# Transposing v as 32-bit words of two channels in a cross-covariance attention and highway kernel

## The chip, the cores and the metric

The kernel runs on one core of a Trainium2 chip. A core has TensorE (PE), which multiplies matrices and can transpose, and whose loads of the stationary operand are recorded apart (PEld); VectorE (DVE); ScalarE (ACT); GpSimd (POOL); SyncE (SP), which here only starts transfers; and 16 DMA engines. Each engine works through its own queue in order. The metric is the device time of one execution in microseconds (us), and smaller is better.

## The reference

Four batches, 6336 positions (N), 256 channels (C), everything f32 in memory. Attention is between channels, so its map is only 256 x 256 for each batch, and a highway layer follows.

```python
qn = q / (norm(q, axis=1) + 1e-06)          # norm of each channel over N
kn = k / (norm(k, axis=1) + 1e-06)
a  = softmax(kn.transpose(0, 2, 1) @ qn / tau)   # (B, 256, 256)
x  = (v @ a).reshape(B * N, 256)
H  = maximum(x @ w_h, 0)
T  = sigmoid(x @ w_t + b_t)
out = T * H + (1 - T) * x                   # (25344, 256)
```

## The kernel before

**Tiles.** A batch is 49 tiles of 128 positions and a rest of 64. q, k and v are loaded by POOL-issued transfers that cast f32 to f16, in groups of 2 to 13 tiles (QG, VG), into rings of 4 buffers for q and k each and 3 for v.

**Scores.** For each tile, `emit_score` multiplies k's two halves of channels (stationary, 128 weights each) with all 256 channels of q into a sum S (line 230). The norms are the diagonals of Gram matrices G: k's halves with themselves (line 234) and q's halves with themselves (line 239), two matmuls of 128 columns for each. For some runs of four tiles, listed in RUNS, the sum of squares is made without PE instead (`make_run`): ACT squares (line 448), POOL adds halves (454), DVE reduces (461), and `pe_sums` (511) adds the result to G by an f32 matmul with ones at the end of the batch.

**Chain.** When a batch's scores are complete, `make_chain` goes through norms (502), logits (557), exponentials (574), softmax (588), a transpose of the map, a product with w_h and w_t (618), and copies (629) into `mr`, an f16 tile of 768 columns: for each row, which is a channel of k, the map and its products with w_h and w_t. So x, H's argument and T's argument are all v times a part of `mr`.

**Slots.** An output slot is a pair of position tiles; a batch has 25, the last one with the rest of 64. For each slot PE transposes v, four times 128 x 128 in f16 (line 293, `emit_transpose`), into one PSUM bank (tag vT, a single buffer), DVE or ACT copies it to the SBUF tile `vts` (line 307, or 305 for the slot with the rest; ACT_COPY lists the slots that ACT copies), and `mains` multiplies three times four: `vts` as stationary, 256 columns of `mr` moving (line 317), for the sigmoid's argument (zbank, seeded with the bias by an ACT copy, 361), for H and for x. ACT makes the sigmoid (358), DVE two products (366, 376), POOL most of the final subtractions (399), and stores go out from SP (415) in groups of four slots.

**Order.** A planner in the same file writes the order of every queue: tasks with lengths and dependencies are put on the engines step by step, and the program is emitted in that order. On PE the chain goes first, then scores that are due (S_END, SAHEAD), then transposes up to LOOKS slots ahead, then mains. TAIL says for how many last tiles of a batch Gram products go ahead of scores; QOFF and VOFF how early loads are put in POOL's order; OUTST how many loads may be under way; HOLD how many full output buffers are held back before stores go out; NEAR when DVE prefers a copy; LASTS_AT where the last batch's slot with the rest stands. The lengths that the planner uses for a task (TR, copies) only shape the order.

Of the kernel before, what the change touches and what calls it, by code (L numbers as in the profile page):

```python
# [11 lines left out]
f32 = mybir.dt.float32  # L12
f16 = mybir.dt.float16
u16 = mybir.dt.uint16

P = 128
# [44 lines left out]
def kernel(  # L61
# [11 lines left out]
    nc = tc.nc  # L73

    B, N, C = q.shape
# [11 lines left out]
    def spans(*sizes):  # L87
# [10 lines left out]
    GT = {"q": 12, "k": 12, "v": 13}  # L98
    CH = 4
    SQR = {"q": 4, "k": 2}  # L100
    RUNS = {1: {'q': [4, 8, 20, 32, 36, 44], 'k': [0, 8, 24, 28, 32, 40]}, 2: {'q': [0, 8, 12, 16, 20, 24, 28, 36, 40], 'k': [0, 12, 16, 32, 40]}, 3: {'q': [8, 12, 20, 28, 32, 40, 44], 'k': [0, 8, 16, 28, 32, 36]}}
    TAIL = [6, 12, 10, 7]
    SPARE = 0
    QOFF, VOFF = [1.5, 3.0, 4.0, 0.5], [7.5, 3.5, 0.5, 9.5]
    SAHEAD = [0, 0.5, 10.0, 10.5]
    LOOKS = [3, 3, 2, 2]
    HOLD = [2, 1, 1, 5]
    DVE_SUBS = 2
    SINGLES = 8
    ACT_COPY = {3, 14, 21, 22, 26, 34, 36, 39, 40, 44, 45, 51, 53, 54, 58, 61, 63, 64, 72, 77, 81, 83, 84, 88, 91, 96, 98, 99}  # L110
    NEAR = 2
    OUTST = 7
    QRING, VRING, ORING = 4, 3, 7
    TTR, UXR, VTR = 4, 3, 5
    OG = 4
    LASTS_AT = 18
    LASTS = list(range(LASTS_AT)) + [NPAIR - 1] + list(range(LASTS_AT, NPAIR - 1))
    PAIRS = [list(range(NPAIR))] * (B - 1) + [LASTS]
    S_END = [21.5, 42.5, 65.0]

    ctx.enter_context(tc.manual_schedule())
    const_pool = ctx.enter_context(tc.tile_pool(name="consts", bufs=1))
# [1 line left out]
    work_pool = ctx.enter_context(tc.tile_pool(name="work", bufs=2))  # L124
    psum_pool = ctx.enter_context(
        tc.tile_pool(name="psum", bufs=1, space=bass.MemoryType.PSUM)
    )
# [9 lines left out]
    for t in range(NSLOT):  # L137
        b, i = pair_of(t)
# [13 lines left out]


    MM = lambda n: n / 2376.0 + 0.0025
    EXP_LAG = 0.6
    PE_LAG, LAG, TO_PE = 0.20, 0.08, 0.10
    TILE = 0.309
    STEP, LAND = 0.01, 0.9
# [60 lines left out]
    def emit_score(b, j, parts, first, last):  # L219
        if first:  # L220
            tags = ("S", "G") if b == 0 else ("hx1", "hx2")
            S_t[b] = psum_pool.tile([P, 2, C], f32, tag=tags[0], name=f"S{b}")
            G_t[b] = psum_pool.tile([P, 4, P], f32, tag=tags[1], name=f"G{b}")
        nr = REM if j == NS else P
        kk, qq = tile_of("k", b, j), tile_of("q", b, j)
        S, G = S_t[b], G_t[b]
        for c in range(2):
            kc = kk[0:nr, bass.ts(c, P)]
            if "s" in parts:
                nc.tensor.matmul(  # L230
                    S[:, c, :], kc, qq[0:nr, :], start=first and c == 0, stop=last and c == 1
                )
            if "k" in parts:
                nc.tensor.matmul(  # L234
                    G[:, c, :], kc, kc, start=begins(b), stop=False, skip_group_check=True,
                )
        for c in range(2 if "q" in parts else 0):
            qc = qq[0:nr, bass.ts(c, P)]
            nc.tensor.matmul(  # L239
                G[:, 2 + c, :], qc, qc, start=begins(b), stop=False, skip_group_check=True  # L240
            )
# [42 lines left out]
    vT_ps, vT_t = {}, {}  # L284
    slot_of = {pair_of(t): t for t in range(NSLOT)}

    def emit_transpose(t):
        b, i = pair_of(t)
        ps = psum_pool.tile([P, 2, 2, P], f16, tag="vT", name=f"vtps{t}")
        for u, r in enumerate(nrows(i)):  # L290
            vt = tile_of("v", b, 2 * i + u)
            for c in range(2):
                nc.tensor.transpose(  # L293
                    ps[:, u, c, 0:r], vt[0:r, bass.ts(c, P)], ident[0:r, 0:r]
                )
        vT_ps[t] = ps

    def emit_copy(t, e):
        i = pair_of(t)[1]
        sb = work_pool.tile([P, 2, 2, P], f16, tag="vTs", bufs=VTR, name=f"vts{t}")  # L300
        cp = nc.vector.tensor_copy if e == "DVE" else nc.scalar.copy
        ps = vT_ps.pop(t)
        if i == NPAIR - 1:
            for u, r in enumerate(nrows(i)):
                cp(out=sb[:, u, :, 0:r], in_=ps[:, u, :, 0:r])
        else:
            cp(out=sb, in_=ps)  # L307
        vT_t[t] = sb

    mr_t = {}  # L310

    def mains(t, dst, off, seeded):
        b, i = pair_of(t)
        mr = mr_t[b]
        for u, r in enumerate(nrows(i)):
            for kt in range(2):
                nc.tensor.matmul(  # L317
                    dst[0:r, u, :], vT_t[t][:, u, kt, 0:r], mr[:, kt, off : off + C],
                    start=(not seeded and kt == 0 and (u == 0 or i == NPAIR - 1)),
                    stop=(kt == 1 and (u == 1 or i == NPAIR - 1)),  # L320
                    skip_group_check=seeded,
                )
# [169 lines left out]
    def make_chain(b):  # L492
        st = {}
        T = {}
        def norms(kind):
# [9 lines left out]
                    )  # L505
            return emit

        def pe_sums(e):
            for kind, o in (("q", 2), ("k", 0)):
                for c in range(2 if (kind, b) in sums_t else 0):  # L510
                    nc.tensor.matmul(
                        G_t[b][:, o + c, :],
                        areas[kind][sums_t[kind, b]][:, 0, bass.ts(c, P)], ones32,
                        start=False, stop=True, skip_group_check=True,
                    )

# [202 lines left out]
    for t in range(NSLOT):  # L719
        i = pair_of(t)[1]  # L720
        odd = i == NPAIR - 1
        Z[t] = Task(("Z", t), "PE", 4 * MM(C), lambda e, t=t: mains(t, zbank[t % 2], 2 * C, True))

        def emit_hx(e, t, which):
            task = (H if which == "h" else X)[t]
            hx[which, t] = bank_tile(task, f"{which}{t}")
            mains(t, hx[which, t], C if which == "h" else 0, False)

        H[t] = Task(("H", t), "PE", 4 * MM(C), lambda e, t=t: emit_hx(e, t, "h"))
        X[t] = Task(("X", t), "PE", 4 * MM(C), lambda e, t=t: emit_hx(e, t, "x"))  # L730
        H[t].wants_bank = X[t].wants_bank = True
        H[t].readers = lambda t=t: [TH[t]]
        X[t].readers = lambda t=t: [UX[t]]
        TR[t] = Task(("T", t), "PE", 4 * MM(P), lambda e, t=t: emit_transpose(t))
        CP[t] = Task(("C", t), "any", 0.0, lambda e, t=t: emit_copy(t, e))
        TT[t] = Task(("tt", t), "ACT", 0.61, lambda e, t=t: emit_tt(t))
        SEED[t] = Task(("seed", t), "ACT", 0.61, lambda e, t=t: emit_seed(t))
        TH[t] = Task(("th", t), "DVE", 0.75 if odd else 0.61, lambda e, t=t: emit_th(t))
        UX[t] = Task(("ux", t), "DVE", 0.75 if odd else 0.61, lambda e, t=t: emit_ux(t))
# [247 lines left out]
    def take(n, engine, now, length=None):  # L987
        task = head(n)
        if not can(task, now):
            return False  # L990
        if engine == "PE" and slot_now() == 0 and last_score[0].end is not None:
            if any(t.engine == "DMA" and t.end + LAND + 0.5 > now for t, _ in task.after):
                return False
        ptr[n] += 1
        run(task, engine, now, length)
        return True

    def soon(engine, now, length):
        task = head(engine + ".chain")
        if task is None or task.name[1] not in (0, B - 1):  # L1000
            return False
        if any(t.end is None for t, _ in task.after):
            return False
        return max(t.end + lag for t, lag in task.after) < now + length
# [31 lines left out]
    def step_act(now):  # L1036
        for n in ("ACT.chain", "ACT.tt", "ACT.seed"):
            if (n != "ACT.tt" or not exp_table()) and take(n, "ACT", now):
                return True
        wait = slot_now() == 0 and soon("ACT", now, 0.58)  # L1040
        if not wait and ptr["copy"] in ACT_COPY and take("copy", "ACT", now, 0.58):
            return True
        return slot_now() > 0 and not soon("ACT", now, 1.05) and take("ACT.sq", "ACT", now)

    def step_dve(now):
        if take("DVE.chain", "DVE", now):
            return True
        if slot_now() == 0 and soon("DVE", now, 0.42):
            return False
        mine = ptr["copy"] not in ACT_COPY  # L1050
        if mine and ptr["copy"] - slot_now() < NEAR and take("copy", "DVE", now, 0.42):
            return True
        if take("DVE.thux", "DVE", now) or take("DVE.sub", "DVE", now):
            return True
        if mine and take("copy", "DVE", now, 0.42):
            return True
        return slot_now() > 0 and not soon("DVE", now, 1.0) and take("DVE.red", "DVE", now)

# [122 lines left out]
```

## Time and profile before

| | |
|---|---|
| median of 3 runs | 270.83 us (270.56 to 274.89) |
| profiled execution | 270.55 us, span 268.8 us |
| PE, PEld busy | 246.3 us (92%), 213.7 us (79%) |
| DVE, ACT, POOL busy | 207.6, 192.9, 206.5 us |
| read from, written to memory | 78.4 MB, 26.0 MB |
| transposes of v (line 293) | 392 of 128x128 and 8 of 64 rows, f16 |
| mains (line 317) | 1200 |
| runs of squares (line 448) | 39, 1055 ns each on ACT |

PE is one of TensorE's rows, PEld the other; they overlap. A busy row says when an engine was at work, not that it was at its peak: matmuls are pipelined, and what one costs is the distance of its start from the next. A group's line ends in busy us, mean ns of one, and the idle time before it with what ended it. The DMA line gives the mean busy share of the 16 DMA engines in tenths.

### The profile page before, as it was taken

What the parts mean: (1) busy time and instruction counts of PE and PEld (TensorE: products, weight loads), DVE (VectorE), ACT (ScalarE), POOL (GpSimd) and SP (SyncE); (2) the same over time, 40 slices, a digit from 0 to 9 for tenths busy, and PEclk for the clock granted to TensorE, in tenths of its full rate; (3) what the DMA queues carried; (4) which work ended last, traced back from release to release, by engine and by line L of the source; (5) the groups of instructions that cost most, each with busy time, mean ns of one, the idle gap of its engine ahead of it and who ended that gap; (6) DMA issues with size and microseconds to landing.
All of it is one profiled execution on the core that took longest, in us unless ns stands there. A gap on an engine that the chain in (4) does not pass through costs nothing.

```text
span 268.8 us, 6452 instructions
## 1 busy us (share of the span) xinstructions
PE 246.3 (92%) x2564; PEld 213.7 (79%) x2564; DVE 207.6 (77%) x414; ACT 192.9 (72%) x320; POOL 206.5 (77%) x183
## 2 busy tenths in 40 slices
PE   0996886999999999989999999999999999999990
PEld 0696784798889997879989987898988687999780
DVE  2000035869999999889989899889998998999894
ACT  3310025969689978879996798898868987888780
POOL 6133455399989999898899998899966485977880
PEclk9999999999999999999999999999999999999998
DMA  7999999999999999999999999999999999698435
GB/s 215 213 214 212 205 186 212 214 209 220 213 210 213 235 266 220 209 274 213 288 290 307 278 213 226 214 297 302 272 291 356 266 408 399 142 235 355 200 129 215
DMA packets 16143, 66.08 MB, mean 246 GB/s; under 512 B 1777, under 2 KB 4338, under 8 KB 13170
## 3 DMA queue, kind: packets, MB, share of 16 engines
q0 software_dynamic: 11040, 38.67, 73.0%
q1 hardware_dynamic: 4786, 26.22, 24.3%
q10 hardware_dynamic: 288, 0.79, 0.8%
q8 instruction: 20, 0.33, 0.4%
q14 instruction: 9, 0.07, 0.1%
HBM read 78.38 MB, written 25.95 MB: 388 GB/s over the span
## 4 chain that ended last, share of the span: by engine, by line
PE 47%; DMA 29%; POOL 9%; DVE 7%; ACT 3%; issue 3%; DVEq 0%; POOLq 0%; ACTq 0%
DMA k<-in_k_dram 24%; PE x L317 10%; PE h L317 9%; PE zbank L317 9%; PE S L230 7%; PE vtps L293 5%; POOL o L399 4%; DMA out_dram<-o 3%; PE G L234 3%; PE G L239 3%; DVE o L366 2%; DMA qk<-in_k_dram 2%; DVE ux L376 2%; ACT tt L358 1%; POOL q L177 1%
## 5 line engine op out<-in xcount | busy, mean ns | idle before, releaser
L399 POOL TENSOR_TENSOR o<-o,ux 128x1024 f32<-128x1024 f32 (+2 forms) x50 | 111.5, 2233 | 23.4 <-DVE ux L376 20.3
L317 PEld LDWEIGHTS <-vts 128*128 128x128 f16 x1200 | 111.7, 98 | 16.2 <-issue 4.1
L230 PE MATMUL S<-q,k 128*128 128x256 f16 x392 | 73.5, 278 | 12.5 <-ACT k L834 6.3
L358 ACT ACTIVATE tt<-zbank 128x512 f32<-128x512 f32 x100 | 59.4, 596 | 22.0 <-PE zbank L317 15.7
L366 DVE SCALAR_TENSOR_TENSOR o<-h,tt 128x512 f32<-128x512 f32 x96 | 65.6, 684 | 6.0 <-ACT tt L358 3.3
L376 DVE SCALAR_TENSOR_TENSOR ux<-tt,x 128x512 f32<-128x512 f32 (+1 forms) x104 | 68.0, 657 | 2.1 <-PE x L317 2.0
L317 PE MATMUL x<-mr,vts 128*128 128x256 f16 (+1 forms) x400 | 60.5, 273 | 0.3 <-DVE o L366 0.3
L317 PE MATMUL zbank<-mr,vts 128*128 128x256 f16 (+1 forms) x400 | 60.6, 273 | 0.0
L317 PE MATMUL h<-mr,vts 128*128 128x256 f16 (+1 forms) x400 | 60.5, 273 | 0.0
L361 ACT COPY zbank<-btb 128x512 f32<-128x512 f32 x98 | 57.6, 591 | 2.7
L230 PEld LDWEIGHTS <-k 128*128 128x128 f16 x392 | 37.5, 100 | 18.9 <-DMA k<-in_k_dram 7.8
L234 PE MATMUL G<-k 128*128 128x128 f16 x256 | 44.0, 224 | 0.7 <-DVE junk L502 0.7
L293 PE MATMUL vtps<-ident,v 128*128 128x128 f16 x392 | 38.3, 219 | 1.5 <-DVE vts L307 0.7
L307 DVE COPY vts<-vtps 128x512 f16<-128x512 f16 x68 | 28.6, 420 | 7.2 <-PE vtps L293 6.7
L293 PEld LDWEIGHTS <-v 128*128 128x128 f16 x392 | 28.7, 98 | 4.9 <-issue 1.7
L177 POOL DMA_DIRECT2D q<-in_q_dram x25 | 14.2, 570 | 23.0 <-PE G L239 18.6
L502 DVE SCALAR_TENSOR_TENSOR junk<-G,ident 128x128 f32<-128x128 f32 x16 | 4.7, 291 | 31.1 <-PE G L234 30.4
L239 PE MATMUL G<-q 128*128 128x128 f16 x216 | 28.6, 224 | 0.0
L454 POOL TENSOR_TENSOR sqq<-sqq 128x512 f32<-128x512 f32 (+1 forms) x22 | 26.5, 1207 | 0.1
L234 PEld LDWEIGHTS <-k 128*128 128x128 f16 x256 | 24.0, 101 | 1.8 <-issue 1.1
L448 ACT ACTIVATE sqq<-q 128x1024 f32<-128x1024 f16 x22 | 23.0, 1055 | 0.1
L461 DVE TENSOR_REDUCE sqq<-sqq 128x256 f32<-128x768 f32 x22 | 22.6, 1026 | 0.0
(78 smaller groups left out, 214.3 us busy)
## 6 DMA issues: line engine op xcount, KB each, us to landing
out_dram<-o SPq DMA_DIRECT2D x23, 1024.0 KB, 9.8
v<-in_v_dram POOLq DMA_DIRECT2D x11, 768.0 KB, 17.2
q<-in_q_dram POOLq DMA_DIRECT2D x7, 768.0 KB, 15.2
k<-in_k_dram POOLq DMA_DIRECT2D x7, 768.0 KB, 19.3
q<-in_q_dram POOLq DMA_DIRECT2D x9, 512.0 KB, 13.4
k<-in_k_dram POOLq DMA_DIRECT2D x9, 512.0 KB, 15.4
v<-in_v_dram POOLq DMA_DIRECT2D x4, 832.0 KB, 19.1
q<-in_q_dram POOLq DMA_DIRECT2D x4, 256.0 KB, 13.2
```

The lines of the kernel that those rows point to most:

```text
L230: nc.tensor.matmul(S[:, c, :], kc, qq[0:nr, :], start=first and c == 0, stop=last and c == 1)
L234: nc.tensor.matmul(G[:, c, :], kc, kc, start=begins(b), stop=False, skip_group_check=True,)
L239: nc.tensor.matmul(G[:, 2 + c, :], qc, qc, start=begins(b), stop=False, skip_group_check=True)
L293: nc.tensor.transpose(ps[:, u, c, 0:r], vt[0:r, bass.ts(c, P)], ident[0:r, 0:r])
L307: cp(out=sb, in_=ps)
L317: nc.tensor.matmul(dst[0:r, u, :], vT_t[t][:, u, kt, 0:r], mr[:, kt, off : off + C], start=(not seeded and kt == 0 and (u == 0 or i == NPA ...
L358: nc.scalar.activation(out=tts[t], in_=zbank[t % 2], func=Act.Sigmoid)
L361: nc.scalar.copy(out=zbank[t % 2], in_=btb)
L366: nc.vector.scalar_tensor_tensor(out=ot[pr, o0 + us.start : o0 + us.stop, :], in0=hx["h", t][pr, us, :], scalar=0.0, in1=tts[t][pr, us, :] ...
L376: nc.vector.scalar_tensor_tensor(out=uxs[n][pr, 2 * half + us.start : 2 * half + us.stop, :], in0=tts[t][pr, us, :], scalar=1.0, in1=hx["x ...
L399: ins = sub.tensor_tensor(out=dst, in0=dst, in1=uxs[n][pr, us, :], op=AluOp.subtract)
L454: nc.gpsimd.tensor_tensor(out=sq[:, 1 : 1 + half, :], in0=sq[:, 1 : 1 + half, :], in1=sq[:, 1 + CH - half : 1 + CH, :], op=AluOp.add,)
```

## The change

v's f16 tile is read as 32-bit words, each of two neighbouring channels, and transposed by f32 transposes with the f32 identity `ident0`: one 128 x 128 transpose for each position tile instead of two. A row of the result then belongs to a channel pair, and a position's two channels lie side by side. The copy moves 256 f32 words instead of 512 f16 values, and its result is viewed as f16 again. The mains read their stationary operand with a step of two elements, and contract over even channels first, then odd ones. So that `mr` has its rows in that order, k's channels are taken with a step of two in the scores and Grams and in the sums of squares. RUNS lists 30 runs instead of 39 (by the change's own title 27). Planner constants are others: lengths of transposes and copies, and all that places work.

```diff
-    RUNS = {1: {'q': [4, 8, 20, 32, 36, 44], 'k': [0, 8, 24, 28, 32, 40]}, 2: {'q': [0, 8, 12, 16, 20, 24, 28, 36, 40], 'k': [0, 12, 16, 32, 40]}, 3: {'q': [8, 12, 20, 28, 32, 40, 44], 'k': [0, 8, 16, 28, 32, 36]}}
-    TAIL = [6, 12, 10, 7]
+    RUNS = {1: {'q': [4, 8, 20, 32, 36, 44], 'k': [24, 28, 32]}, 2: {'q': [16, 20, 24, 36], 'k': [8, 12, 16, 36, 40]}, 3: {'q': [8, 12, 16, 28, 32], 'k': [0, 8, 16, 24, 28, 36, 40]}}
+    TAIL = [7, 11, 12, 3]
-    QOFF, VOFF = [1.5, 3.0, 4.0, 0.5], [7.5, 3.5, 0.5, 9.5]
-    SAHEAD = [0, 0.5, 10.0, 10.5]
+    QOFF, VOFF = [0.5, 4.0, 3.5, 0], [7.0, 4.0, 1.0, 6.0]
+    SAHEAD = [0, 2.5, 8.0, 11.5]
-    HOLD = [2, 1, 1, 5]
+    HOLD = [1, 1, 1, 2]
-    ACT_COPY = {3, 14, 21, 22, 26, 34, 36, 39, 40, 44, 45, 51, 53, 54, 58, 61, 63, 64, 72, 77, 81, 83, 84, 88, 91, 96, 98, 99}
-    NEAR = 2
-    OUTST = 7
+    ACT_COPY = {0, 4, 5, 7, 8, 11, 15, 19, 21, 25, 27, 33, 34, 35, 42, 53, 57, 60, 63, 74, 76, 77, 80, 83, 86, 87, 89, 92, 93, 95, 97, 99}
+    NEAR = 3
+    OUTST = 8
-    LASTS_AT = 18
+    LASTS_AT = 16
-    S_END = [21.5, 42.5, 65.0]
+    S_END = [22.0, 42.0, 66.0]
-    EXP_LAG = 0.6
+    EXP_LAG = 0.0
@@ emit_score
-            kc = kk[0:nr, bass.ts(c, P)]
+            kc = kk[0:nr, :].rearrange("p (i two) -> p two i", two=2)[:, c, :]
@@ emit_transpose
-        ps = psum_pool.tile([P, 2, 2, P], f16, tag="vT", name=f"vtps{t}")
+        ps = psum_pool.tile([P, 2, P], f32, tag="vT", name=f"vtps{t}")
-            for c in range(2):
-                nc.tensor.transpose(
-                    ps[:, u, c, 0:r], vt[0:r, bass.ts(c, P)], ident[0:r, 0:r]
-                )
+            nc.tensor.transpose(ps[:, u, 0:r], vt[0:r, :].bitcast(f32), ident0[0:r, 0:r])
@@ emit_copy
-        sb = work_pool.tile([P, 2, 2, P], f16, tag="vTs", bufs=VTR, name=f"vts{t}")
+        sb = work_pool.tile([P, 2, P], f32, tag="vTs", bufs=VTR, name=f"vts{t}")
-        vT_t[t] = sb
+        vT_t[t] = sb.bitcast(f16).rearrange("p u (r c) -> p u r c", c=2)
@@ mains
-                    dst[0:r, u, :], vT_t[t][:, u, kt, 0:r], mr[:, kt, off : off + C],
+                    dst[0:r, u, :], vT_t[t][:, u, 0:r, kt], mr[:, kt, off : off + C],
@@ make_chain, pe_sums
+        def channels(ap, kind, c):
+            if kind == "q":
+                return ap[:, bass.ts(c, P)]
+            return ap.rearrange("p (i two) -> p two i", two=2)[:, c, :]
-                        areas[kind][sums_t[kind, b]][:, 0, bass.ts(c, P)], ones32,
+                        channels(areas[kind][sums_t[kind, b]][:, 0, :], kind, c), ones32,
@@ the planner's lengths
-        TR[t] = Task(("T", t), "PE", 4 * MM(P), lambda e, t=t: emit_transpose(t))
+        TR[t] = Task(("T", t), "PE", 2 * MM(P), lambda e, t=t: emit_transpose(t))
-        if not wait and ptr["copy"] in ACT_COPY and take("copy", "ACT", now, 0.58):
+        if not wait and ptr["copy"] in ACT_COPY and take("copy", "ACT", now, 0.42):
-        if mine and take("copy", "DVE", now, 0.42):
+        if mine and take("copy", "DVE", now, 0.34):
```

More of the change, by code (lines that the diff above doesn't have):

```diff
@@ L304, in emit_copy @@
             for u, r in enumerate(nrows(i)):
-                cp(out=sb[:, u, :, 0:r], in_=ps[:, u, :, 0:r])
+                cp(out=sb[:, u, 0:r], in_=ps[:, u, 0:r])
         else:
             cp(out=sb, in_=ps)
-        vT_t[t] = sb
+        vT_t[t] = sb.bitcast(f16).rearrange("p u (r c) -> p u r c", c=2)
     mr_t = {}
@@ L1039, in step_act @@
                 return True
-        wait = slot_now() == 0 and soon("ACT", now, 0.58)
-        if not wait and ptr["copy"] in ACT_COPY and take("copy", "ACT", now, 0.58):
+        wait = slot_now() == 0 and soon("ACT", now, 0.42)
+        if not wait and ptr["copy"] in ACT_COPY and take("copy", "ACT", now, 0.42):
             return True
@@ L1050, in step_dve @@
         mine = ptr["copy"] not in ACT_COPY
-        if mine and ptr["copy"] - slot_now() < NEAR and take("copy", "DVE", now, 0.42):
+        if mine and ptr["copy"] - slot_now() < NEAR and take("copy", "DVE", now, 0.34):
             return True
```

## The prediction

> **What bounds the kernel now.** I read the page's first two blocks first, then busy time by stage, then TensorE's timeline, then the groups by shape.
>
> The page's totals, and two of its 40-slice lines:
>
> ```profile
> PE 246.3 (92%) x2564; PEld 213.7 (79%) x2564; DVE 207.6 (77%) x414; ACT 192.9 (72%) x320; POOL 206.5 (77%) x183
> ...
> PE   0996886999999999989999999999999999999990
> ...
> DMA  7999999999999999999999999999999999698435
> ```
>
> Two resources are full. From slice 8 on (about 53 us) TensorE (PE) is dense to 262 us; the DMA engines are full from slice 2 to slice 34, then half used. The same by stage (columns: stretch, its length, busy us and instructions of PE, weight loads, DVE, ACT, POOL, clock, DMA share, GB/s):
>
> ```profile
> 53.00:204.00 151.00, 148.46 (x1577) 131.42 (x1578) 138.91 (x260) 126.22 (x201) 142.07 (x117) 1.00 1.05 249
> ...
> 212.00:250.00 38.00, 38.00 (x382) 33.08 (x381) 35.69 (x69) 32.37 (x57) 28.86 (x16) 1.00 0.90 302
> 250.00:262.60 12.60, 12.54 (x120) 9.92 (x117) 11.42 (x25) 9.57 (x17) 10.54 (x9) 1.00 0.44 170
> ```
>
> PE is idle 2.5 of 151 us and 0.1 of 50.6. Busy time alone could hide bubbles, since each matmul is recorded longer than its pitch, so I priced a slot from the timeline (start, us covered):
>
> ```profile
> 229.45 0.39 PE L293 MATMUL vtps<-ident,v 128*128 128x128 f16 x4
> 229.67 0.60 PE L317 MATMUL zbank<-mr,vts 128*128 128x256 f16 x4
> ...
> 230.98 0.39 PE L293 MATMUL vtps<-ident,v 128*128 128x128 f16 x4
> ```
>
> One slot is 1.53 us: four transposes take 229.67 - 229.45 = 0.22 us (56 ns each), twelve mains 1.31 us (109 ns each). Pricing all 2564 matmuls so (f32 ones at 111, below) gives 234 us of real work, 199 of it in the 209.6 us from 53 to 262.6. PE's own work sets the end there.
>
> Is DMA as binding? Loads alone run at 213 GB/s (slices 2 to 4), stores alone at up to 408. 38.67 MB / 213 + 26.22 MB / 408 = 182 + 64 = 246 us, so some 17 of the last 65 us are unused. The last batch's map is the test: its last copy (line 629) starts at 212.6, and its first slot at 223.5. Seven older slots stand in front, so DMA can let PE finish some 10 us earlier. For the two maps before, that reserve is 1 and 5 us.
>
> [...]The trace has no f32 transpose, but f32 matmuls:
>
> ```profile
> 93.46 0.60 PE L317 MATMUL zbank<-mr,vts 128*128 128x256 f16 x4
> 93.90 0.61 PE L511 MATMUL G<-ones,sqq 128*128 128x128 f32 x4
> 94.34 0.61 PE L511 MATMUL G<-ones,sqk 128*128 128x128 f32 x4
> 94.79 0.39 PE L293 MATMUL vtps<-ident,v 128*128 128x128 f16 x4
> ```
>
> Two calls of 128 columns are four instructions in 0.44 us: 111 ns each, 222 a call. A quarter of that is 56 ns, an f16 transpose's pitch. [...]f16 loads take 98 ns, f32 loads 192. [...]
>
> ```profile
> L307 DVE COPY vts<-vtps 128x512 f16<-128x512 f16 x68 | 28.6, 420 | 7.2 <-PE vtps L293 6.7
> L307 ACT COPY vts<-vtps 128x512 f16<-128x512 f16 x28 | 16.3, 582 | 3.7 <-PE vtps L293 3.6
> ...
> L610 DVE CAST at_sb<-at 128x256 f16<-128x256 f32 x4 | 1.7, 423 | 0.4 <-PE at L599 0.4
> L610 ACT CAST at_sb<-at 128x256 f16<-128x256 f32 x4 | 1.5, 372 | 2.6 <-PE at L599 2.6
> ```
>
> 256 f32 words cost DVE 423 ns, the 512 halves 420; ACT saves 582 - 372 = 210.[...]
>
> **The change part by part**, priced on PE.
>
> Transposes: 392 full-size f16 become 196 f32. At 56 ns, a slot saves 2 x 56 = 0.112 us, 11.1 over 100 slots. What the new one costs is the unknown. [...]From above: 222, two passes as the f32 matmuls have. Between: the f32 load limits it. The first of a pair loads under the preceding 109 ns main, as the f32 load at 93.9 did; the second waits about 111, so a slot takes 167 instead of 222 ns. I take 56.
>
> Where it counts: five or six slots run before 53 us, where PE waits for loads (-0.6 lost), and in the last eight, DVE and the chain of copies and sigmoids is nearly late (-0.9 lost): there DVE's pitch is 0.60 + 0.60 + 0.34 for each copy it makes, 1.42 a slot, beside PE's new 1.42. So -9.6 us.
>
> Runs of squares: the lists hold 39 before and 30 after (the 27 of the change's title is not what the diff has). Nine removed runs free 9 x 1.06 ACT, 9 x 1.28 POOL, 9 x 1.03 DVE, none of which sets the end, and put 9 x 4 tiles x 2 Gram matmuls = 72 x 56 ns = 4.0 us on PE, all after 53 us. +4.0. Each of those also holds PE's queue: what stands behind it are mains and transposes, and behind those DVE and ACT.
>
> Copies: DVE still makes 68 or so at an unchanged 0.42; ACT makes 32 at about 0.37 for 28 at 0.58 (16.3 to 11.9, -4.4 us). One bank holds the transposes (tag vT), so the next waits for this copy; that is 0.7 us of PE waits in all now. 0 on PE; if ACT's cover were gone, -4.4 at the most.
>
> Strided reads: 1200 loads of vts and about 680 of k, and k as moving operand in the Grams. From below 0 (no reason for a gain). From above: a load [...]111 ns as in f32, adds 2 ns behind 109 ns mains (2.4 us) and 55 behind each of 280 k Gram matmuls (15.4 us). I take 0. The sums' f32 weights (line 511), 12 half-loads for k: under 1 us.
>
> Places: the load order (QOFF, VOFF), stores (HOLD), SAHEAD, TAIL, OUTST move. Loads pass POOL's subtractions and squares' adds; each issue holds POOL 0.55 us, count unchanged; stores stay on SP. DMA has no room before 204, so a worse order costs PE idle time at a map: that is 2.5 us between 53 and 204 now. Bounds -2 to +6; I take 0.
>
> Sum: -9.6 + 4.0 = **-5.6 us** on the profiled 270.55 (span 268.8 + 1.75), 264.95; the median of the runs is 270.83, 0.28 more. **265 us.** Late next are DVE in the tail and the last map: with seven slots in front shrunk by 5 us, DMA's reserve covers it.
>
> **The rivals.** *The f32 load limits.* For: f32 loads take 192, and 111 is their pitch. [...]PE: -5.5 + 0.7 + 4.0 = -0.8: **270 us**, no change.
>
> *Slower: the array drains at each change of mode.* The trace shows such a price at other shapes. In the chain of waits, a group of four mains, and two groups with 64-wide weights:
>
> ```profile
> 220.84 0.44 PE x L317 x4
> ...
> 222.05 0.66 PE h L317 x4
> 222.71 0.66 PE x L317 x4
> ```
>
> 0.22 more: at entry and at exit [...]96 ns each. If the f32 transpose mode needs that, each slot pays 0.19, 100 of them 19 us: -5.6 + 19.2 = +13.6, **284 us**. It decides once a slot's pair costs over 0.18 us in all (0.22 less the Grams' 0.04). Against: f16 to f32 at 93.90 drains nothing.
>
> *Two passes* [...]: 444 a slot, +22.2 + 4.0: **297**. *Strides lose the fast load*: -5.6 + 15.4 = +9.8: **280**. *The places fit worse*: 268 to 275.
>
> **The numbers.** Forecast 36% (its own range 262 to 268), load-limited 24%, drain 15%, places 10%, two passes 8%, strides 7%. 2% is about what a measurement of this kernel can tell from no change, and it lies at 265.4, just above my forecast: two thirds of the first case and a little of the places are faster (0.28); the rest of it, the load-limited case and half of the places the same (0.40); what remains is slower (0.32). For 8 in 10 I leave out the two passes and the drain case's larger part: 261 to 282.
>
> **What would show it.** Right: line 293 halved to some 200 instructions, four mains starting 0.11 us after a pair began; a slot of 1.42 us in the tail; weight loads of vts still near 98 ns; DVE copies at 0.42, ACT's at 0.37. Load-limited: 0.17 per pair, second matmul 111 after the first. Drain: mains starting some 0.2 us late after each pair. Two passes: 392 instructions again. Strides: line 234's pitch over 56 ns, loads over 98. Wrong also if PE stays dense but the last map comes later than 218 us.

## The result, and the profile after

The changed kernel takes 277.56 us (median; 277.16 to 278.05) where the kernel before takes 270.81 beside it. The ratio is 1.025, its 95% interval 1.023 to 1.028: **2.5% slower, +6.75 us**, where 265.0 was forecast. The time is inside the range of 261 to 282, the sign is wrong. That the range holds is luck: it reached so high for the strides (280) and for part of the drain (284), and neither is what happened. The profiled execution took 277.69 us, its span 275.9.

The page after: totals, and three of the 40-slice lines (a slice is now 6.9 us).

```profile
PE 252.4 (91%) x2436; PEld 219.0 (79%) x2436; DVE 199.3 (72%) x400; ACT 182.4 (66%) x316; POOL 195.8 (71%) x174
...
PE   0997887999999999999999999959999899999990
...
PEclk9999999999999999999999999997999999999996
DMA  7999999999999999999999999999997969997534
```

DVE, ACT and POOL have 8.3, 10.5 and 10.7 us less to do, and nothing of that reached the end. PE's row rose by 6.1 us with 128 instructions fewer. And there is a hole: slice 26 is half empty on PE, and in the slice after it the granted clock falls to 0.7 (PEclk, the clock that TensorE was given, in tenths of full speed).

The groups by shape of the kernel after answer most of what the prediction asked about single instructions.

```profile
L292 PE MATMUL vtps<-ident,v 128*128 128x128 f32 x196 | 38.8, 278 | 0.5 <-DMA v<-in_v_dram 0.3
L304 DVE COPY vts<-vtps 128x256 f32<-128x256 f32 x65 | 27.4, 421 | 11.5 <-PE vtps L292 11.4
...
L292 PEld LDWEIGHTS vtps<-ident,v 128*128 128x128 f32 x196 | 22.9, 142 | 3.4 <-issue 0.8 <-DVE vts L304 0.7 <-DVE mr L631 0.5
L304 ACT COPY vts<-vtps 128x256 f32<-128x256 f32 x31 | 11.4, 368 | 8.1 <-PE vtps L292 8.0
...
L314 PEld LDWEIGHTS <-vts 128*128 128x128 f16 x1176 | 113.7, 98 | 18.1 <-issue 5.2
```

Transposes are halved, 196 instructions for 392, so there are not two passes. But one is recorded at 278 ns, like a matmul of 256 f16 columns (279 ns in the group of line 230). The loads of `vts` take 98 ns under a stride of two, as before without it. DVE's copy takes 421 ns, ACT's 368: both as forecast.

The pitch of the transposes is in PE's timeline after, in the tail (start, us covered):

```profile
240.87 0.38 PE L292 MATMUL vtps<-ident,v 128*128 128x128 f32 x2
241.09 0.60 PE L314 MATMUL zbank<-mr,vts 128*128 128x256 f16 x4
...
242.40 0.38 PE L292 MATMUL vtps<-ident,v 128*128 128x128 f32 x2
```

A pair takes 241.09 - 240.87 = 0.22 us, 109 ns each, and a slot 242.40 - 240.87 = 1.53 us, the same as before. For its 128 columns an f32 transpose took 109 ns where an f16 one took 56: two of them cost PE what four f16 ones did, 0.22 us. The main behind starts on time, 109 ns after the second transpose, so nothing shows here of the 0.19 us a slot that the drain rival counted.

By stage, in the same columns as the prediction's table of the kernel before:

```profile
53.00:204.00 151.00, 147.06 (x1449) 129.88 (x1447) 126.22 (x236) 113.46 (x186) 126.46 (x105) 0.99 1.04 242
212.00:250.00 38.00, 37.23 (x322) 31.25 (x321) 34.41 (x73) 32.63 (x63) 27.02 (x16) 1.00 0.92 284
250.00:269.30 19.30, 19.24 (x168) 16.01 (x166) 17.34 (x34) 15.54 (x29) 15.66 (x11) 1.00 0.53 214
```

In the same 151 us PE gets through 1449 matmuls instead of 1577. Transposes make 126 of these 128 (118 for 244); 22 mains, 12 scores and 8 of the f32 sums are fewer, which come later, and 40 Gram products more. The starts of slots place the loss (numbering slots from 0): slot 25 starts at 109.7 before and 109.0 after, slot 50 at 169.8 and 170.5, slot 75, the first of the last batch, at 223.5 and 230.4; PE ends at 262.5 and 269.2. **Slot 25 to 50 is 1.4 us slower, slot 50 to 75 is 6.1 us slower, and the last 25 slots take 39.0 us before, 38.8 after.** The last map's product with w_h and w_t is late too, 218.1 against 211.6.

What is in that stretch shows in PE's timeline after (what ended an idle time stands in brackets):

```profile
182.34 0.39 PE L292 MATMUL vtps<-ident,v 128*128 128x128 f32 x2
185.96 0.87 PE L314 MATMUL x<-mr,vts 128*128 128x256 f16 x4 [3.23 <-DVE o L363]
...
187.47 1.06 PE L314 MATMUL zbank<-mr,vts 128*128 128x256 f16 x4
188.33 1.06 PE L314 MATMUL h<-mr,vts 128*128 128x256 f16 x4
...
191.02 0.60 PE L314 MATMUL zbank<-mr,vts 128*128 128x256 f16 x4
191.46 0.60 PE L314 MATMUL h<-mr,vts 128*128 128x256 f16 x4
```

PE waits 3.23 us for DVE's product `o`. DVE's timeline, and the chain of waits, say why:

```profile
185.21 0.69 DVE L363 SCALAR_TENSOR_TENSOR o<-h,tt 128x512 f32<-128x512 f32 x1 [3.88 <-DMA out_dram<-o]
```

```profile
173.53 1.42 POOL ol L396 x2
174.96 0.02 issue
174.97 10.12 DMA out_dram<-o
...
185.21 0.70 DVE o L363
...
185.96 0.87 PE x L314 x4
```

DVE cannot write its next product, because the output tile that it needs (there is a ring of seven) has not been stored yet. The store that frees one was released at 174.97 by a POOL subtraction and needed 10.12 us beside the loads. Before, the chain has such a store too, issued at 172.54 and done in 8.87, and PE waited 0.26 us at 182.25:

```profile
172.54 8.87 DMA out_dram<-o
```

```profile
182.25 0.60 PE L317 MATMUL x<-mr,vts 128*128 128x256 f16 x4 [0.26 <-DVE o L366]
```

Behind the longer pause, mains run at twice their pitch: four in 188.33 - 187.47 = 0.86 us, against 191.46 - 191.02 = 0.44. The windows of that stretch, of the kernel before and then of the kernel after:

```profile
180.00:192.00 12.00, 11.74 (x127) 10.57 (x125) 11.18 (x20) 10.21 (x17) 11.71 (x9) 1.00 1.04 303
```

```profile
180.00:192.00 12.00, 8.77 (x69) 7.23 (x68) 6.56 (x11) 5.95 (x10) 8.97 (x7) 0.86 1.03 307
```

The granted clock is 0.86 over these 12 us, for 1.00 before; from 186.14 to 189.55 it is 0.50. DMA is as busy as before (1.03 for 1.04). With the 3.2 us of waiting and some 1.7 us of slow matmuls (185.96 to 191.02 for what takes 3.4 us at the pitches seen elsewhere), this one place holds about 5 of the 6.1 us.

### The profile page after: what moved, and what is told of

It reads as the page before. It is cut to its first block, busy times and chain, and to the rows that moved or that the text cites. A ratio compares the mean times of both kernels' runs of the same rounds, so it can differ in the third digit from the quotient of the medians.

```text
span 275.9 us, 6177 instructions
## 1 busy us (share of the span) xinstructions
PE 252.4 (91%) x2436; PEld 219.0 (79%) x2436; DVE 199.3 (72%) x400; ACT 182.4 (66%) x316; POOL 195.8 (71%) x174
## 4 chain that ended last, share of the span: by engine, by line
PE 74%; DMA 15%; DVE 4%; ACT 2%; POOL 1%; issue 1%; DVEq 0%; ACTq 0%
PE h L314 14%; PE x L314 14%; PE zbank L314 14%; PE S L230 13%; DMA k<-in_k_dram 10%; PE vtps L292 7%; PE G L234 4%; PE G L239 4%; DMA out_dram<-o 4%; DMA qk<-in_k_dram 2%; DVE ux L373 1%; PE ah L620 1%; PE G L513 1%; DVE o L363 1%; DVE mr L590 1%
## 5 line engine op out<-in xcount | busy, mean ns | idle before, releaser
L314 PEld LDWEIGHTS <-vts 128*128 128x128 f16 (+1 forms) x1200 | 115.4, 99 | 20.6 <-issue 7.7
L230 PEld LDWEIGHTS <-k 128*128 128x128 f16 x392 | 38.4, 100 | 16.2 <-ACT k L836 6.4
L234 PE MATMUL G<-k 128*128 128x128 f16 x272 | 48.0, 225 | 0.7 <-DVE junk L499 0.7
L292 PE MATMUL vtps<-ident,v 128*128 128x128 f32 x196 | 38.8, 278 | 0.5 <-DMA v<-in_v_dram 0.3
L304 DVE COPY vts<-vtps 128x256 f32<-128x256 f32 x65 | 27.4, 421 | 11.5 <-PE vtps L292 11.4
L239 PE MATMUL G<-q 128*128 128x128 f16 x272 | 35.4, 224 | 0.0
L234 PEld LDWEIGHTS <-k 128*128 128x128 f16 x272 | 25.6, 100 | 1.7 <-issue 1.1
L292 PEld LDWEIGHTS vtps<-ident,v 128*128 128x128 f32 x196 | 22.9, 142 | 3.4 <-issue 0.8
L239 PEld LDWEIGHTS <-q 128*128 128x128 f16 x272 | 22.5, 100 | 2.3
L451 POOL TENSOR_TENSOR sqk<-sqk 128x512 f32<-128x512 f32 (+1 forms) x15 | 17.4, 1168 | 0.8 <-ACT sqk L445 0.8
L451 POOL TENSOR_TENSOR sqq<-sqq 128x512 f32<-128x512 f32 (+1 forms) x15 | 17.3, 1167 | 0.0
```

The lines of the kernel that those rows point to most:

```text
L230: nc.tensor.matmul(S[:, c, :], kc, qq[0:nr, :], start=first and c == 0, stop=last and c == 1)
L234: nc.tensor.matmul(G[:, c, :], kc, kc, start=begins(b), stop=False, skip_group_check=True,)
L239: nc.tensor.matmul(G[:, 2 + c, :], qc, qc, start=begins(b), stop=False, skip_group_check=True)
L292: nc.tensor.transpose(ps[:, u, 0:r], vt[0:r, :].bitcast(f32), ident0[0:r, 0:r])
L314: nc.tensor.matmul(dst[0:r, u, :], vT_t[t][:, u, 0:r, kt], mr[:, kt, off : off + C], start=(not seeded and kt == 0 and (u == 0 or i == NPA ...
L451: nc.gpsimd.tensor_tensor(out=sq[:, 1 : 1 + half, :], in0=sq[:, 1 : 1 + half, :], in1=sq[:, 1 + CH - half : 1 + CH, :], op=AluOp.add,)
```

## The experiments

What had to be told apart: (a) that the transposes are worth nothing; (b) that the Grams are PE work at the end, as forecast; (c) that the places and the stall are to blame; and, when a first answer failed, (d) whether PE's work sets the end at all. "Slot 75" below is when the last batch's first slot starts: 223.5 us before, 230.4 after. Each time has the kernel before beside it; its medians lay between 270.74 and 271.39.

**E1: only the transposes, the strides and the copies**, in the kernel before: of the change's diff the parts under emit_score, emit_transpose, emit_copy, mains, make_chain and pe_sums. Its runs, places and lengths stay, and each engine works in the order of before.

> The kernel before with f32 transposes and channels by stride alone; runs of squares, places and planner lengths as before, so the order of every queue is that of before. Theory (an f32 transpose streams at half the column rate, a pair costs 0.218 us where four f16 ones cost 0.222, and strides cost nothing): PE work falls by 0.4 us, ACT loses 28 x 0.21 = 6 us of copies that were hidden; 269.5 to 271.5 us, no change. Rival (the f32 mode or the strides are what costs the 7 us, through waits that the pitch doesn't show): 275 to 278 us.

Measured: 270.92 us, ratio 0.999 (0.996 to 1.002). Its page's totals and its transposes:

```profile
PE 246.3 (92%) x2364; PEld 213.2 (79%) x2364; DVE 207.5 (77%) x414; ACT 188.5 (70%) x320; POOL 206.6 (77%) x183
```

```profile
L292 PE MATMUL vtps<-ident,v 128*128 128x128 f32 x196 | 38.4, 276 | 0.9 <-DVE vts L304 0.8
```

PE is busy for 246.3 us, to the tenth what it was, with 200 instructions fewer. So transposes, strided reads and smaller copies together are worth nothing, between -1.0 and +0.5 us by the interval. The 6.75 us then come from the runs and the places. (The new runs and places with the old f16 transposes were not run; that the f32 transposes cost more in the new order than in the old is not excluded.)

**E2: only the list of runs** of the changed kernel, in the kernel before: the RUNS line of the change's diff and nothing else.

> The kernel before with the changed list of 30 runs alone; f16 transposes and all other places as before. Theory: 72 more Gram matmuls of 56 ns on a full PE, 4.0 us: 274 to 276 us. Rival (the freed ACT, POOL and DVE time pays for it, or DMA sets the end): 270 to 272 us.

Measured: 279.94, ratio 1.031 (1.025 to 1.037): +8.5 us, twice the 4.0. PE's work by pitches is 237.7 us, the 4.0 more that was reckoned; the rest is idle time, pauses of 2.8 us at 145 and 2.0 at 166 among it, and slower matmuls behind the second (four f16 transposes in 0.43 us at 168.36, for 0.22 at 148.45); slot 75 comes at 234.4. With these runs the planner writes another order, and that order fits worse. The runs alone are therefore no clean measure of the Grams.

**E8: the Grams alone, order unchanged.** Nine runs keep their squares, sums and places, and their Gram products are made besides, in `emit_score`, so that those norms count their tiles twice.

```diff
+    AGAIN = {1: {"k": [0, 8, 24]}, 2: {"q": [0, 8, 12, 16, 28]}, 3: {"q": [8]}}
...
+        if "s" in parts:
+            parts += "".join(x for x in "kq" if (x, b, j) in again)
```

> The kernel before with 72 more Gram matmuls, those of nine of its runs of squares, put beside the scores of the same tiles; the runs are still made on ACT, POOL and DVE and the written order is unchanged (those norms count the tiles twice, so the output differs). Theory (Gram matmuls cost a full PE 56 ns each, and the 8.5 us of the run with the shorter list alone had more in it: an order that fits less well): +4.0 us, 274.3 to 275.5. Rival (72 Grams are worth 7 us or more through the weight loads and waits around them): 277 to 280 us. Rival (another engine sets the end): 271 us.

Measured: 273.00, ratio 1.006 (1.003 to 1.008): +1.5 us by the ratio (1.9 by the medians) for 4.0 us of PE work. Slot 75 comes at 225.9, 2.4 late, and the last map's product at 213.9, 2.3 late. It lies between the two theories: PE's work counts in part.

**E3: the planner's length for the transposes.** The change halves it in the plan, though it didn't halve in fact; here it is set back.

```diff
-        TR[t] = Task(("T", t), "PE", 2 * MM(P), lambda e, t=t: emit_transpose(t))
+        TR[t] = Task(("T", t), "PE", 4 * MM(P), lambda e, t=t: emit_transpose(t))
```

> The changed kernel with the planner's length for a slot's transposes set to what they cost in the trace, 4 x MM(128) = 0.225 us, in place of 0.113; the work is the same, only the written order differs. Theory (the 3.2 us stall on a full ring of output tiles at 182 us and the slower clock after it come from a plan that has PE 0.11 us per slot too fast): the stall goes, 271 to 274.5 us. Rival (the places themselves hold stores too long): the stall stays, 276 to 278 us.

Measured: 277.89, ratio 1.024 (1.018 to 1.031): nothing gained, and the theory of a wrong length fell. The stall at 182 is gone, but others stand elsewhere (2.0 us at 214 and 1.3 at 53), with the same end. Removing the one stall that the trace shows was not removing the loss.

**E4: the changed kernel with the 39 runs of before.** The edit of E2 turned round.

> The changed kernel with the list of 39 runs of the kernel before. Theory: 72 Grams less on PE, -4.0 us, with the places otherwise as changed: 272 to 275 us. Rival (the places alone make the 7 us): 276 to 279 us.

Measured: 274.06, ratio 1.011 (1.007 to 1.014). So in the new places the runs cost 3.5 us, and with the old runs the new places still cost 3.0. The stall at 182 is gone from its trace (PE waits 0.2 us for `o` there), and the granted clock is 0.995 over the span, for 0.986 in the changed kernel.

**E6: stores earlier.** In the changed kernel a store is tied to POOL's subtraction before the last one issued, instead of to the last.

```diff
-            last_pool[0] = h
+            last_pool[0] = subs[-1] if subs else h
+            subs.append(h)
```

> The changed kernel with each held store tied to the subtraction before the one that the planner tied it to, some 2.5 to 5 us earlier; the order of every queue is the same. Theory (the 3.2 us wait for a store at 182 us and the half clock after it are 5 us of the loss): the wait goes, 271.5 to 274 us. Rival (stores that go earlier only put loads later, and the last batch's map with them): 276 to 279 us.

Measured: 274.01, ratio 1.011 (1.008 to 1.014): 3.5 us back. PE's wait falls from 3.23 to 1.23 us, in PE's timeline of E6:

```profile
183.52 0.60 PE L314 MATMUL x<-mr,vts 128*128 128x256 f16 x4 [1.23 <-DVE o L363]
```

The mains behind it cover 0.60 us and the granted clock is 1.00 over 180 to 192, so the fall of the clock is gone as well, and slot 75 is at 226.6. The edit moves every held store, but 3.3 us of the gain lie where the stall was: slot 50 to 75 takes 56.6 us for 59.9. For the changed kernel the stall is a cause of its loss, about half of it.

**E12 and E13: is an earlier store good as such?** E12 puts E6's edit into E1, E13 into E4.

> The kernel before with the f32 transposes and strides, and held stores tied one subtraction earlier; all work done. Theory: its waits for stores are small (1.5 us on DVE before), so little is to be had: 269.5 to 271.5 us. Rival (stores are late in this order too): 267 to 269 us, faster than both kernels.

> The changed kernel with the list of 39 runs of before and with held stores tied one subtraction earlier: the two edits that each gave 3.5 us, together. Theory (Grams on PE and late stores are two separate costs and together the whole loss): 270 to 272 us. Rival (both act on the same wait, the last batch's map, or what was left belongs to other places): 273 to 275 us.

Measured: E12 272.54, ratio 1.006 (1.004 to 1.007), slower than E1 by some 1.7 us; E13 273.97, ratio 1.011, the same as E4 and as E6. Earlier stores help only the order that has this stall, and the two gains of 3.5 do not add: both take away the same loss.

**E14 and E15: which of the places?** The changed kernel with 39 runs (E4) gets back the old values of one half of its constants: QOFF, VOFF, SAHEAD, HOLD, OUTST and S_END in E14; TAIL, ACT_COPY, NEAR, LASTS_AT, EXP_LAG and the planner's lengths in E15.

> The changed kernel with 39 runs and the constants that place loads, stores and scores (QOFF, VOFF, SAHEAD, HOLD, OUTST, S_END) as before; TAIL, ACT_COPY, NEAR, LASTS_AT, EXP_LAG and the planner's lengths as changed. Theory (the 3.2 us that the places cost beside the runs lie in when loads and stores go out, since DMA is full): 270 to 272 us. Rival (they lie in who copies when, and the lengths): 273.5 to 275 us.

> The changed kernel with 39 runs, and TAIL, ACT_COPY, NEAR, LASTS_AT, EXP_LAG and the planner's lengths as before; the constants that place loads, stores and scores as changed. Theory (the cost lies in loads and stores): 273.5 to 275 us. Rival (it lies in copies and lengths): 270 to 272 us.

Measured: E14 278.94, ratio 1.028 (1.021 to 1.034); E15 275.24, ratio 1.012 (1.006 to 1.018). Put back together, both halves give E1's 270.9; each alone gives no gain on E4's 274.1, and E14 is 4.9 us worse. Their traces have new places like the one at 182: in E14 waits of 2.1 and 2.0 us at 160 and 216, in E15 a wait of 1.95 us for `o` at 184, and granted clocks of 0.972 and 0.984 over their spans, for E4's 0.995. The constants are fitted to each other. Which of them costs the last 3 us cannot be said from halves, and stays open; E4's trace shows only that PE waits for DVE there in the chains of the maps, 1.3 us at 104 and 1.4 at 163.

**E5 and E7: had the forecast's transpose been real.** E5 leaves every second transpose out, and the copy spreads the one that is left over both tiles of the slot, so that the second is computed from the first one's v. A pair then costs 0.109 us, the 0.112 of the forecast; E7 adds E6's edit.

```diff
-            nc.tensor.transpose(ps[:, u, 0:r], vt[0:r, :].bitcast(f32), ident0[0:r, 0:r])
+            if u == 0 or r < P:
+                nc.tensor.transpose(ps[:, u, 0:r], vt[0:r, :].bitcast(f32), ident0[0:r, 0:r])
...
-            cp(out=sb, in_=ps)
+            cp(out=sb, in_=ps[:, 0:1, :].to_broadcast([P, 2, P]))
```

> The changed kernel with one f32 transpose for a slot in place of two; the copy spreads that one over both halves, so the second position tile of a slot is computed from the first one's v. A slot's transposes then cost PE 0.109 us, which is what the prediction took for the pair and what the plan has. Theory (only the price of the pair was wrong, the rest of the sum holds): PE has 10.7 us less work, the stall goes because the plan fits, and the time is what was predicted, 263 to 267 us. Rival (DMA or another engine sets the end whatever PE does): 270 us or more; rival (the stall is independent of PE): 266 to 269 us.

> Both: one f32 transpose for a slot (the second position tile of a slot is computed from the first one's v) and the held stores tied one subtraction earlier. Theory (with the price and without the stall the sum of the prediction holds): 264 to 268 us. Rival (DMA and the last map at 214 us set the end): 270 to 273 us.

Measured: E5 272.02, ratio 1.003 (1.000 to 1.006); E7 269.97, ratio 0.997 (0.995 to 0.999). Even at the forecast's price the change would have been no gain, and with E6's edit one of 0.3%. Less work on PE leaves the stall where it was, in PE's timeline of E5:

```profile
178.66 0.28 PE L293 MATMUL vtps<-ident,v 128*128 128x128 f32 x1
183.11 1.01 PE L315 MATMUL x<-mr,vts 128*128 128x256 f16 x4 [4.17 <-DVE o L364]
```

PE comes to the full output tiles earlier and waits longer, 4.17 us for 3.23. This broke the forecast's first premise, and asked for (d).

**E9, E10, E11: PE's work, the transfers, or both.** All start from E1, with the old runs and order. E9 leaves out every second transpose as E5 does (10.9 us of PE work). E10 stores only the first half of each group's rows; its page has 13.4 MB written for 26.0, 12.6 MB less:

```diff
-            parts = [(rows(ob)[:, 2 * i0 : 2 * (i0 + n), :], ot[:, o0 : o0 + 2 * n, :])]
+            parts = [(rows(ob)[:, 2 * i0 : 2 * i0 + n, :], ot[:, o0 : o0 + n, :])]
```

E11 does both.

> The kernel before with the f32 transposes and strides (39 runs, order of before), and one transpose for a slot in place of two (the second position tile of a slot is computed from the first one's v): PE has 10.9 us less work. Theory (until the last batch's first slot, at 223.5 us, DMA and the ring of seven output tiles set the pace, so only the last 25 slots gain, 25 x 0.109): 267.5 to 269 us. Rival (PE's own work sets the end, as the prediction had it): 260 to 263 us.

> The kernel before with the f32 transposes and strides (39 runs, order of before), and each store of a group writes only the first half of its rows: 12.8 MB less for DMA, 31 us at 408 GB/s; PE's work is the same. Theory (PE and DMA are both nearly full, each would set nearly the same end alone): PE then sets it, 266 to 270 us. Rival (DMA alone sets the end): 255 to 262 us. Rival (PE alone sets it): 270 to 271.5 us.

> Both: one transpose for a slot in place of two, and half of each store left out, same order of every queue. Theory (two full resources): the gain is more than the sum of the two alone, 256 to 262 us. Rival (the ring and DMA have nothing to do with it; the order's own waits hold the rest): the sum of the two alone, 265 us or more.

| kernel | left out | median us | ratio (95%) | us against before |
|---|---|---|---|---|
| E9 | 10.9 us of PE work | 267.84 | 0.988 (0.980 to 0.996) | -2.9 |
| E10 | 12.6 MB of stores | 269.20 | 0.994 (0.993 to 0.996) | -1.5 |
| E11 | both | 263.80 | 0.971 (0.965 to 0.977) | -6.9 |

Of 10.9 us taken from PE, some 3 arrive. With the stores halved too, the ratio falls by 2.9% (2.3 to 3.5), more than the 1.2 + 0.6 = 1.8% of the two alone, though by the width of E9's interval only just. The traces say it more clearly. From slot 0 to slot 75, where E9 has 8.2 us less work for PE, it takes 177.3 us before, 177.3 in E9, 176.7 in E10 and 171.5 in E11: there neither gives as much as 1 us alone in these traces, and both together 5.8 us. Each limits what the other is worth. E11 missed the lower times expected of it; its transfers still fill DMA through slice 27 (183 us), as its DMA line shows:

```profile
DMA  7999999999999999999999999999775972496231
```

Where E9's work went is in its waits. The lines of the kernel before, then of E9 (waited for: us in total, times, longest):

```profile
PE S L230 <- DMA k<-in_k_dram: 6.2, 7, 1.4
...
DVE o L366 <- DMA out_dram<-o: 1.5, 2, 0.8
```

```profile
PE S L230 <- DMA k<-in_k_dram: 8.9, 8, 2.0
...
DVE o L364 <- DMA out_dram<-o: 3.5, 2, 2.4
```

The scores wait longer for k, and DVE for a free output tile. Between slots 0 and 75 PE's waits for k and `o` make 6.6 us in E9 and 2.3 before; the 4.3 us more are about half of the 8.2, the rest is in smaller waits. In E9's profiled execution, the slowest of its four at 270.46, slot 75 starts at 225.5, later than before; but its slot 0 is 2.0 us late already. That would account for most of the 2.5 to 3.2 us by which the other three executions, which have no trace, ended sooner. In this trace only the last 25 slots, where transfers have room, run faster: PE's timeline of E9 there has slots of 236.76 - 235.34 = 1.42 us instead of 1.53.

```profile
235.34 0.27 PE L293 MATMUL vtps<-ident,v 128*128 128x128 f32 x1
235.45 0.60 PE L315 MATMUL zbank<-mr,vts 128*128 128x256 f16 x4
...
236.76 0.27 PE L293 MATMUL vtps<-ident,v 128*128 128x128 f32 x1
```

From slot 75's start to slot 99's it takes 260.2 - 225.5 = 34.7 us, the kernel before 260.6 - 223.5 = 37.1. No kernel here that does all of the work was faster than the kernel before.

## Why the prediction was wrong

**Bounds: "PE's own work sets the end" failed.** By E9 it holds for the last 25 slots only. Up to the last batch's first slot, PE and the transfers are both full, and E9 shows that PE's work taken away there returns as waits, about half of it for k and for output tiles. The prediction asked whether DMA could be earlier, and read a reserve of "some 10 us" off the last map's copy standing 10.9 us ahead of its slot. That reserve is of k and of the map, and E9's trace made no use of it: the last map's product came at 213.9, for 211.6 before. It says nothing of the output tiles, which fill when slots run ahead of the stores. Nor was PE as dense as read: the prediction's own sum, 199 us of work in 209.6, leaves 10 us. The 0.26 us wait on `o` at 182 in the trace of before was a sign, and was not read. By E9's -2.9, this step alone would have turned -9.6 into about -3.

**The f32 transpose: taken at 56 ns, measured 109.** One instruction, as taken, but 109 ns for its 128 columns. It lies between the 56 taken and the upper bound of 222, but no rival had it: the load-limited one had 167 ns for a pair that takes 0.22 us. The second load of a pair is not what sets it: in E9 a single transpose between mains, with no f32 load behind it, still takes 235.45 - 235.34 = 0.11 us. The 56 was not shown: the trace of before has that pitch for f16 transposes alone, and of f32 only matmuls, at 222 ns a call; 222 to 109 is a factor of two. With 109 the first term of the sum goes from -9.6 to about -0.4; with 4.0 for the Grams that is 274 us, slower and not faster.

**The Grams: +4.0 taken.** The PE work is right: by pitches (f16 transposes 56 ns, f32 ones and mains 109), real work went from 233.7 to some 237.3 us. What it costs is not: 1.5 us at an unchanged order (E8), 3.5 in the new places (E4), 8.5 in the old ones (E2). "All after 53 us", so all of it counted, is the same false premise as above, and a new list of runs is also a new order.

**The places: 0 taken, bounds -2 to +6.** They cost 3.0 with 39 runs (E4), inside the bounds, and with the new runs a stall of 3.2 us and a fall of the clock to 0.50 behind it. The prediction looked for the cost at the maps, as waits for loads; the part that is shown, the stall, came from the stores and the ring of output tiles. What makes up the 3.0 is open, and E4's trace has waits at the maps, though for DVE and not for loads. "Stores stay on SP" was true and not enough: SP waits for POOL's subtraction, and for DMA.

**Right:** strided reads at nearly 0 (98 ns loads, 109 ns mains; only k's Grams, which also stream k with the step, rose from a pitch of 56 to 58 ns, some 0.6 us on 280 of them), no drain (the main starts 109 ns after the second f32 transpose), DVE's copy unchanged at 0.42 and ACT's at 0.37, and no gain from freeing DVE, ACT and POOL. A last map after 218 us was named as a sign of being wrong: its product came at 218.1. Of the rivals, "the places fit worse" (268 to 275) is the nearest in its cause, with its size too small since it still counted the transposes' gain; the 280 of the strides is nearer in number only. **The actual path**, as far as it is shown: transposes and strides 0 (E1), runs and places 6.7 together; either's share depends on which is put in first (E2, E4).

## What to carry to other kernels

Where two resources are full, price what is taken from one only in the stages where the other has room, and ask for every buffer in between, the output ring too, how long until it is full. An instruction that no row of the profile shows deserves its whole span between the bounds, and a forecast should be worked through at the worse end too. And an order that a planner fitted to its constants is one piece: here one half of the constants moved the time by 8 us with the same runs and the same work (E14 against E1), more than the operation that the change was about.

## What was not expected of the hardware

- A 128 x 128 f32 transpose was one instruction of 109 ns pitch with a load of 142 ns in the kernel after; an f32 matmul of 128 columns in the kernel before was two of 111 ns each, with loads of 192.
- After PE had waited 3.23 us, mains ran at half their rate (0.86 us for four, against 0.44), with a granted clock of 0.50 from 186.14 to 189.55 us and of 1.00 from there to 192. After 4.17 us in E5 four mains took 185.41 - 184.56 = 0.85 us, with a granted clock of 0.86 over 178 to 190; after 1.23 us in E6 the mains kept their pitch, and the clock was 1.00 over 180 to 192.
- In E2, after a wait of 2.75 us that ended at 148.34, four f16 transposes took 148.67 - 148.45 = 0.22 us, as elsewhere; after one of 2.04 us that ended at 167.85, they took 168.79 - 168.36 = 0.43. No run varied the length of a pause by itself, so what decides between the two is open.
